# Two expert layers: unused single units load no weights, four leave the main run for a conditional block

## The chip, the core and the metric

The program runs on one core of one Trainium2 chip. The metric is device time in microseconds (us) of one execution. The core has five engines with queues of their own: TensorE (PE; its weight loads are listed as PEld), VectorE (DVE), ScalarE (ACT), GpSimd (POOL) and SyncE (SP). SP issues the plain transfers, POOL the indirect ones. An engine works through its queue in order and waits on semaphores.

## What is computed

Windowed attention, then two expert layers, on 7168 tokens of width 192. Layer one sends each token to two of eight experts, layer two to one.

```python
def reference(**kwargs):
    attn_out = _attn_ref(**attn_kwargs)             # seven last tokens, weights by softmax
    x = attn_out.reshape(B * S, D)
    x = _moe_ref(x=x, **moe_kwargs)                 # two experts a token, noisy gate
    return _moe2_ref(x=x, **moe2_kwargs)            # one expert a token, cosine router
...
            h = np.maximum(x[mask] @ w1[e], 0.0)    # 192 -> 1024
            out[mask] += top2_w[mask, k, None] * (h @ w2[e])   # 1024 -> 192
```

Which tokens an expert gets is known only on the chip. The reference's own routing of its inputs gives the experts of layer one 1867, 1722, 1777, 1820, 1775, 1810, 1732 and 1833 entries, those of layer two 1184, 1182, 2138, 279, 462, 463, 585 and 875.

## The kernel before

**Units.** A unit is 128 entries of one expert. Two units of one expert make a pair, and a tile of work is a pair or a single unit. The number of tiles is fixed when the program is built, with room for every routing: layer one has 56 pair slots and 8 single units, layer two 28 and 8. A single unit is for an expert with an odd number of units (or for a pair that found no slot). With the counts above the experts' units are 15, 14, 14, 15, 14, 15, 14, 15 and 10, 10, 17, 3, 4, 4, 5, 7. Each layer thus has four experts with an odd number and fills its pair slots (56 and 28) with the rest: units 0 to 3 of each layer hold entries, units 4 to 7 are computed on rows that are thrown away when they are written.

**A tile's steps.** `gather` (POOL, three tiles ahead) fetches the rows. `weights` (SP) fetches the expert's weights from DRAM (`WS`, names ws0 and ws1 for the two layers) in two parts: part 0, 4096 columns or 1024 KB, for the first product, and part 1, 3072 columns or 768 KB, for the second. `transp` turns the rows on PE. `first_product` (line L1028 in the profile, tile `ph`) is 40 matmuls, each of 256 columns in a pair and of 128 in a single unit. ACT and DVE make the hidden layer's two halves `hh` and `hl`. `second_product` (L1054, tile `py`) is 48 matmuls, or 24 in a single unit. ACT scales the result into `ys`, POOL scatters it. The first product of a tile is interleaved with the second of the tile before (`ORDER`).

**Weights and buffers.** Pairs use two buffers by turns, `wb[0]` and `wb[1]` (in the trace `wb`). All single units of both layers share a third that lies in the end of the input's tile (in the trace `xh`; its loads are the rows `xh<-ws`). Every load carries a condition, the integer `flag_i` of its slot:

```python
            e = SP.value_load(exec_i[l][0:1, c:c + 1], min_val=0, max_val=7)
            f = SP.value_load(flag_i[l][0:1, c:c + 1], min_val=0, max_val=1)
            loads.append(SP.dma_start(w[:, cols], WS[l][bass.ds(e * 128, 128), cols], cond=f))
```

For a pair the flag is one where its buffer passes to another expert. For all eight single units it is one (L688). `issue_after` keeps the loads in the order of the code, so a load that waits for its buffer holds up all later ones.

**Order.** `Layer` writes out the order of the tiles. Slots run in sections, as entries become known; the single units stand in the last section that still mixes all token groups, one behind each of its first eight pairs.

**Beside the tiles.** Routing, and the preparation of layer two's weights (L276 to L281 load `in_moe2_w1`, `in_moe2_w2` into a part of `xh`; L340 to L346 store them as ws1), are issued between the tiles by points in the program; their transfers share SP's queue with the loads. Tile i of the whole program is the i-th of layer one's 64 and layer two's 36.

Of the kernel before, what the change touches and what calls it, by code (L numbers as in the profile page):

```python
# [24 lines left out]
NS = 8  # L25
CB = 8
# [13 lines left out]
class Layer:  # L40
    """Static plan of one routed layer: k entries per token, column groups of tokens."""

    def __init__(self, k, groups, mixed):
        self.k, self.groups = k, groups
        self.np = N * k // 256
        self.cap = [b * 128 * k // 256 for _, b in groups]
        self.sec = [0] + [cdiv(b * 128 * k - E * 255, 256) for _, b in groups[:-1]]
        # mixed: the slot by which the entries of all groups but the last have been run
        self.done = [(groups[-2][1] * 128 * k + E * 255) // 256] if mixed else []
        # Each run of slots is taken from its start and from its middle by turns, one weight buffer for either,  # L50
        # so that a buffer is loaded anew only where its own half passes on to another expert.
        cuts = self.sec + self.done + [self.np]
        self.buf, self.fresh, order = {}, [], []
        for a, b in zip(cuts, cuts[1:]):
            m = a + cdiv(b - a, 2)
            self.fresh += [a, m]
            u = 0
            for j in range(b - a):
                s = (a, m)[j % 2] + j // 2
                self.buf[s] = len(self.buf) % 2  # L60
                order.append(("p", s))
                # the single units follow the first pairs that hold entries of every group
                left = NS - j
                if a == self.sec[-1] and 0 < left <= NS:
                    order.append(("s", u))
                    u += 1
        assert len(order) == self.np + NS
        self.order = order
        self.pos = {o: i for i, o in enumerate(order)}
        self.first = [self.pos[("p", s)] for s in self.sec]  # L70
        self.units = 2 * self.np + NS


@with_exitstack
def two_moe(ctx: ExitStack, tc: tile.TileContext, x, wgen, w_gate, w_noise, noise, w1a, w2a, emb, tau, w1b, w2b, out):
    nc = tc.nc
    L1 = Layer(2, G1, True)
    L2 = Layer(1, G2, False)
# [71 lines left out]
    # masks by partition: all, below 64, from 64 on  # L150
# [9 lines left out]
    # an entry's value: (1 + partition / 128) 2^(place - 56)  # L160
# [94 lines left out]
    @contextmanager  # L255
    def urgent(l):
        """work of a patient job that would wait for ever on an engine that is never idle."""
        low = tc.cur_priority
        if l:
            tc.cur_priority = state["here"]  # L260
        yield
        if l:
            state["here"] = tc.cur_priority
            tc.cur_priority = low
# [108 lines left out]
    def after_tile():  # L373
        """work beside a tile that stays behind the tile's own work that was issued before."""
        return tc.issue_after(state["pin"].ins) if "pin" in state else ExitStack()

    def after_product():
        """TensorE's work beside the tiles, which stays behind the products that were issued before."""
        return tc.issue_after(state["pe"].ins) if "pe" in state else ExitStack()
# [116 lines left out]
    def top1(v, m, dst, n):  # L496
        """dst: one-hot of the first largest of v; m: the largest."""
        t = rt.tile([128, E * GM], F32, name="rowt").rearrange("p (c e) -> p c e", e=E)[:, :n]
        mx = rt.tile([128, GM], F32, name="t1m")[:, :n]
        V.tensor_reduce(m, v, axis=AX.X, op=ALU.max)  # L500
        V.tensor_tensor(t, v, m[:, :, None].to_broadcast([128, n, E]), op=ALU.is_equal)
        yield 0.7
        V.tensor_mul(t, t, desc[:, None, :].to_broadcast([128, n, E]))
        V.tensor_reduce(mx, t, axis=AX.X, op=ALU.max)
        V.tensor_tensor(dst, t, mx[:, :, None].to_broadcast([128, n, E]), op=ALU.is_equal)
        yield 1.0
# [121 lines left out]
    def add_phase(l, lo, hi, at=None):  # L628
        """the pairs lo .. hi of every expert get the slots from `at` on, or those behind the phase before."""
        pn = plan[l]  # L630
        i = pn["rows"]
        w, inc = tn(f"w{l}{i}"), pn["end"][:, i]
        if lo is None:
            V.tensor_copy(w, hi)
        else:
            V.tensor_sub(w, hi, lo)
        prefix(inc, w)
        d = tn(f"d{l}{i}")
        V.tensor_sub(d, inc, w)
        base = float(at) if at is not None else pn["tail"]  # L640
        if base is not None:
            V.tensor_scalar(inc, inc, base, None, op0=ALU.add)
            V.tensor_scalar(d, d, base, None, op0=ALU.add)
        if lo is not None:
            V.tensor_sub(d, d, lo)
        V.tensor_scalar(d, d, 256.0, None, op0=ALU.mult)
        if lo is not None:
            df, cu = tn(f"df{l}{i}"), tn(f"cu{l}{i}")
            V.tensor_sub(df, d, tn(f"d{l}{pn['last']}"))
            V.tensor_scalar(cu, lo, 256.0, None, op0=ALU.mult)  # L650
        pn["last"], pn["tail"], pn["rows"] = i, inc[:, 7:8], i + 1
        return i

    def slot_experts(l, s0, s1):
        """the experts of pair slots s0..s1 (float)."""
        yield from threshold(l, iof[:, s0:s1], s1 - s0, exec_e[l][:, s0:s1])
# [20 lines left out]
    def exec_tables(l, a, b):  # L677
        """integer tables of the slots a..b: the expert, and whether the weights have to be loaded."""
        L = (L1, L2)[l]
        e, ei, fi = exec_e[l], exec_i[l], flag_i[l]  # L680
        V.tensor_copy(ei[:, a:b], e[:, a:b])
        c = min(b, L.np)
        V.tensor_tensor(fi[:, a + 1:c], e[:, a + 1:c], e[:, a:c - 1], op=ALU.not_equal)
        for s in L.fresh:
            if a <= s < c:
                V.memset(fi[:, s:s + 1], 1)
        if c < b:
            V.memset(fi[:, c:b], 1)  # L688
        yield 0.5
# [14 lines left out]
    def rows_of(dst, r, t, sh, phases, l, n):  # L704
        """rows of the ranks r of every expert, in the given phases."""
# [21 lines left out]
    def list_gen(l, L, g, row, n, nu, u0):  # L727
        """the entries of group g by row: onehots of a row's unit and place, multiplied."""
# [57 lines left out]
    def decode(l, v, n, us):  # L786
        """v: integers as floats, 128 (place + 71) + partition, or 0."""
# [20 lines left out]
    def left_over(l, L, g, lrow, fb, u0, nu):  # L808
        """adds the units that the section before g kept: full pairs in their place, and the rest, at the rows lrow."""
# [20 lines left out]
    def section_open(l, L, g, key):  # L830
        """full pairs of the tokens so far run; the rest of each expert is kept behind the last slot."""
# [48 lines left out]
    def left_ranks(l, g):  # L880
        """the ranks at which the two units begin that section g keeps of every expert."""
# [6 lines left out]
    def section_last(l, L, key):  # L888
# [11 lines left out]
        if L.done:  # L900
            # the pairs that end the entries of the groups before stand first
# [17 lines left out]
        def tables():  # L919
# [9 lines left out]
            yield 1.2  # L929
# [34 lines left out]
    live = {}  # L964

    def run_by(b):
        """the tile of layer one by which all entries of the tokens below column b have been run."""
# [15 lines left out]
    def slot(i):  # L983
        """a tile's place in the tables of its layer, and the weights it uses."""
# [3 lines left out]
    def weights(i, part):  # L988
        """part 0: the first product's weights, part 1: the second's."""
# [23 lines left out]
    def first_product(i, bg):  # L1013
        """in four parts, taken by turns with those of the second product of the tile before."""
# [137 lines left out]
    class Job:  # L1152
        """A generator of work with its key, the tile it may start after, and its place in the order of issue."""
# [15 lines left out]
    class Queue:  # L1169
        """Work beside the tiles: chains go one step a point, threads as far as their share of VectorE goes."""  # L1170
# [112 lines left out]
    for i in range(nt):  # L1283
        if i + LA < nt:
# [3 lines left out]
        one = first_product(i + 1, bgq.point) if i + 1 < nt else iter(())  # L1288
# [6 lines left out]
        if i + 3 < nt:  # L1295
            weights(i + 3, 0)
        bgq.at = i + 1
        if i + 2 < nt:
            weights(i + 2, 1)
        if i == C_AT:  # L1300
# [3 lines left out]
            state["last"] = True  # L1304

# [29 lines left out]
```

## Time and profile before

| | |
|---|---|
| time, median of 3 runs | 1094.52 us (1091.99 to 1097.86) |
| span of the profiled execution | 1096.0 us |
| PE busy | 946.8 us (86% of the span) |
| PEld busy | 853.9 us (78%) |
| DVE, ACT, POOL busy | 700.7, 605.3, 407.3 us |
| moved by DMA | 251.81 MB, mean 230 GB/s |
| mean granted clock of PE | 0.950 |

The table gives shares over the whole span. The program has stages with different limits (attention at the start, layer one, a passage in which layer one's results become layer two's inputs, layer two), so a share says little about one of them. The profiled execution has no time of its own on record beside its span; it lies 1.5 us above the median of the timed runs.

### The profile page before, as it was taken

Reading aid. Unit: us, or ns where it says so; the run is one execution under the profiler, and the core shown is the slowest. Engines: PE = TensorE matmul, PEld = TensorE weight load, DVE = VectorE, ACT = ScalarE, POOL = GpSimd, SP = SyncE. Lnnn points to the kernel's source line nnn. Section 1 sums busy time; section 2 is a strip of 40 time slices with the busy share of each in tenths; the row PEclk is TensorE's granted clock in tenths of the full one; section 3 lists DMA queues with packets and bytes.
Section 4 is the critical chain, followed back from the end, with each engine's and each line's share of the span. In section 5 each row is a group of like instructions: output and inputs, shape, how many; then the busy total and the mean of one; then the engine's idle time right before and its main releaser. Section 6 shows DMA issues by size and latency. Waiting matters only on the chain.

```text
span 1096.0 us, 27746 instructions
## 1 busy us (share of the span) xinstructions
PE 946.8 (86%) x10250; PEld 853.9 (78%) x10250; DVE 700.7 (64%) x1943; ACT 605.3 (55%) x1337; POOL 407.3 (37%) x384
## 2 busy tenths in 40 slices
PE   5891259899989999998989998988788999999996
PEld 2551248788878888998979897877678899999896
DVE  8996969889688979553434433988676733333331
ACT  2999336666465765555555543975265344444442
POOL 1000054443445454344334443333344444445422
PEclk9996569999999999999899999999899999999999
DMA  8789674556568564779798977866675736888751
GB/s 269 216 271 293 224 249 143 149 190 200 158 207 285 167 208 142 260 215 329 263 367 292 333 270 229 264 216 180 205 252 160 256 125 217 288 300 306 260 190 41
DMA packets 99464, 251.81 MB, mean 230 GB/s; under 512 B 14207, under 2 KB 65119, under 8 KB 89856
## 3 DMA queue, kind: packets, MB, share of 16 engines
q1 hardware_dynamic: 81664, 215.03, 57.9%
q0 software_dynamic: 17664, 35.01, 11.5%
q8 instruction: 80, 1.31, 0.5%
q14 instruction: 56, 0.46, 0.1%
HBM read 246.09 MB, written 58.69 MB: 278 GB/s over the span
## 4 chain that ended last, share of the span: by engine, by line
PE 32%; DMA 5%; issue 5%; DVE 3%; ACT 3%; POOL 3%; SPq 1%; another core or an unknown queue 1%; POOLq 0%; ACTq 0%
PE ph L1028 15%; PE py L1054 14%; DMA wb<-ws 3%; DMA xh<-ws 2%; PE pt L1006 1%; POOL xg L978 1%; PE bt L468 1%; POOL yb L1062 1%; ACT hh L1030 1%; POOL ss L536 1%; SPq L281 1%; ACT xt L473 1%; ACT xh L448 1%; PE bl L479 1%
## 5 line engine op out<-in xcount | busy, mean ns | idle before, releaser
L1028 PE MATMUL ph<-xt,wb 128*128 128x256 f16 x3360 | 422.6, 276 | 10.0 <-DVE hl L1031 4.1
L1054 PE MATMUL py<-wb,hh 128*128 128x192 f16 x2688 | 361.9, 248 | 17.9 <-ACT ys L1059 13.4
L1030 ACT ACTIVATE hh<-ph 128x512 f16<-128x512 f32 (+1 forms) x400 | 221.4, 560 | 269.7 <-PE ph L1028 209.7
L1028 PEld LDWEIGHTS <-wb 128*128 128x128 f16 x3360 | 327.3, 99 | 47.9 <-issue 9.7
L978 POOL DMA_INDIRECT xg<-t,gx x184 | 196.3, 1067 | 376.0 <-PE pt L1006 157.9
L1054 PEld LDWEIGHTS <-hh 128*128 128x128 f16 x2944 | 266.6, 99 | 28.0 <-issue 18.7
L1031 DVE SCALAR_TENSOR_TENSOR wt<-ph,hh 128x512 f16<-128x512 f32 x200 | 137.4, 689 | 116.6 <-ACT hh L1030 95.2
L1062 POOL DMA_INDIRECT yb<-ys,sx x120 | 131.5, 1096 | 198.0 <-ACT ys L1059 173.9
L1054 PE MATMUL py<-wb,wt 128*128 128x192 f16 x800 | 198.3, 248 | 0.2 <-issue 0.2
L1031 DVE SCALAR_TENSOR_TENSOR hl<-ph,hh 128x512 f16<-128x512 f32 (+1 forms) x200 | 118.9, 603 | 111.2 <-ACT hh L1030 87.6
L1054 PE MATMUL py<-wb,hl 128*128 128x192 f16 x544 | 134.9, 248 | 0.1
L1059 ACT ACTIVATE ys<-py,sc 128x192 f32<-128x192 f32 x184 | 68.0, 415 | 90.1 <-PE py L1054 74.3
L1062 POOL DMA_INDIRECT out_dram<-ys,sx x64 | 64.5, 1007 | 95.6 <-ACT ys L1059 83.5
L385 DVE TENSOR_TENSOR tmp<-xh,wt 128x768 f32<-128x768 f32 x90 | 84.9, 954 | 0.8 <-PE ph L412 0.7
L1054 PEld LDWEIGHTS <-wt 128*128 128x128 f16 x800 | 78.9, 99 | 0.8 <-issue 0.6
L1008 ACT ACTIVATE xt<-pt 128x768 f16<-128x768 f16 x84 | 67.7, 807 | 7.0 <-PE pt L1006 6.9
L1039 DVE TENSOR_SCALAR sc<-xg,csl 128x2 f32<-128x2 f32 (+1 forms) x100 | 23.0, 231 | 75.8 <-ACT ys L1059 60.2
L1054 PEld LDWEIGHTS <-hl 128*128 128x128 f16 x672 | 66.6, 99 | 0.2
L473 ACT ACTIVATE xt<-bt 128x768 f16<-128x768 f16 x56 | 45.2, 807 | 31.8 <-PE bt L468 21.9
L1006 PE MATMUL pt<-identh,xg 128*128 128x128 f16 x552 | 48.7, 222 | 11.6 <-DMA xg<-t,gx 11.4
L1028 PE MATMUL ph<-xt,xh 128*128 128x128 f16 x640 | 45.9, 223 | 7.4 <-DMA xh<-ws 4.7
L1006 PEld LDWEIGHTS <-xg 128*128 128x128 f16 x552 | 39.1, 99 | 14.4 <-DMA xg<-t,gx 11.9
(302 smaller groups left out, 1079.0 us busy)
## 6 DMA issues: line engine op xcount, KB each, us to landing
wb<-ws SPq DMA_DIRECT2D x84, 1024.0 KB
wb<-ws SPq DMA_DIRECT2D x84, 768.0 KB
xh<-ws SPq DMA_DIRECT2D x16, 1024.0 KB
ws<-wo SPq DMA_DIRECT2D x16, 768.0 KB
xh<-ws SPq DMA_DIRECT2D x16, 768.0 KB
tmp<-yb SPq DMA_DIRECT2D x28, 384.0 KB
ws<-wo SPq DMA_DIRECT2D x16, 512.0 KB
ws<-wo SPq DMA_DIRECT2D x32, 256.0 KB
```

The costliest lines, as they stand in the source:

```text
L385: V.tensor_mul(dst.rearrange("p t (h g) -> p (t h) g", g=G), xv, w)
L473: A.activation(xt.rearrange("p a n -> p (a n)"), pa[:, 0:768], AF.Copy)
L978: PL.indirect_dma_start(out=xg[:, h], out_offset=None, in_=T[l][0:rows_in], in_offset=bass.IndirectOffsetOnAxis(ap=gidx[l][:, u + h:u + h ...
L1006: PE.transpose(pt[:, j, h], xg[:, h, 128 * b:128 * b + 128], identh)
L1008: A.activation(xt.rearrange("p j h n -> p (j h n)"), pt.rearrange("p j h n -> p (j h n)"), AF.Copy)
L1028: state["pe"] = mark = PE.matmul(ph[:, q, :n], s, m, start=j == 0, stop=j == 4)
L1030: A.activation(hh[:, fs, :n], ph[:, :, :n], AF.Relu)
L1031: state["pin"] = V.scalar_tensor_tensor(hl[:, fs, :n], ph[:, :, :n], 0.0, hh[:, fs, :n], op0=ALU.max, op1=ALU.subtract)
L1039: V.tensor_scalar(sc[:, :nh], xg[:, :nh, 192:193].bitcast(F32).rearrange("p h o -> p (h o)"), csl[l][:, c:c + 1], None, op0=ALU.mult)
L1054: state["pe"] = PE.matmul(py[:, h], t[:, f, hs], w2[:, f, c], start=f == 0 and j == 0, stop=f == 7 and j == 2)
L1059: A.activation(ys[:, h], py[:, h], AF.Copy, scale=sc[:, h:h + 1])
L1062: d = PL.indirect_dma_start(out=dst, out_offset=bass.IndirectOffsetOnAxis(ap=sidx[l][:, u + h:u + h + 1], axis=0), in_=ys[:, h], in_offset ...
```

## The change

Four things change.

1. The flag of a single unit is computed on the chip: one if the unit holds entries, zero if not (`us`, two small DVE operations more in each layer, and a copy in place of a memset).
2. The single units stand spread over the section, not one behind each of its first pairs. Layer one keeps all eight in the main run, layer two the first four (`KEEP`).
3. Layer two's units 4 to 7 stand behind the main loop in a block that runs only if the flag of unit 4 is one. Inside, nothing is interleaved: gather, loads, transposes and products follow each other, tile by tile.
4. Every engine reads that flag into a register and branches on it. SP reads it earlier: its read stands ahead of part 0 of tile 73 (pair p7 of layer two), 23 tiles before the main run's end.

The order of the last mixed section, p for pairs and s for single units:

```
layer one, before: p33 s0 p40 s1 p34 s2 p41 s3 p35 s4 p42 s5 p36 s6 p43 s7 p37 p44 p38 p45 p39 p46
layer one, after:  p33 p40 s0 p34 p41 s1 p35 s2 p42 p36 s3 p43 s4 p37 p44 s5 p38 s6 p45 p39 s7 p46
layer two, before: p13 s0 p21 s1 p14 s2 p22 s3 p15 s4 p23 s5 p16 s6 p24 s7 p17 p25 p18 p26 p19 p27 p20
layer two, after:  p13 p21 p14 s0 p22 p15 p23 s1 p16 p24 p17 s2 p25 p18 p26 s3 p19 p27 p20 (block: s4 s5 s6 s7)
```

```diff
-                left = NS - j
-                if a == self.sec[-1] and 0 < left <= NS:
+                if a == self.sec[-1] and j + 1 >= cdiv((u + 1) * (b - a), spare + 1) and u < spare:
                     order.append(("s", u))
                     u += 1
+        self.main = len(order)
+        order += [("s", u) for u in range(spare, NS)]
...
-    L1 = Layer(2, G1, True)
-    L2 = Layer(1, G2, False)
+    L1 = Layer(2, G1, True, NS)
+    L2 = Layer(1, G2, False, KEEP)
...
         if c < b:
-            V.memset(fi[:, c:b], 1)
+            V.tensor_copy(fi[:, c:b], tn("us"))
...
+            us = tn("us")
+            V.scalar_tensor_tensor(us, sp, pn["tail"], m8, op0=ALU.is_ge, op1=ALU.mult)
+            V.tensor_scalar(us, us, -1.0, 1.0, op0=ALU.mult, op1=ALU.add)
+            yield 1.6
...
+    nm = base2 + L2.main
...
-    for i in range(nt):
-        if i + LA < nt:
+    for i in range(nm):
+        if i + LA < nm:
...
+    with tc.If(nc.values_load(flag_i[1][0:1, L2.np + KEEP:L2.np + KEEP + 1], min_val=0, max_val=1) > 0):
+        loads.clear()
+        for i in range(nm, nt):
+            gather(i)
+            for part in range(2):
+                weights(i, part)
+            transp(i)
+            for step in (first_product, second_product):
+                for _ in step(i, lambda share: None):
+                    pass
```

**SP in layer one, first place.** Behind the preparation's stores and loads for layer two (ws1, in_moe2_w1) stood, before, part 0 of p34 (wb1), part 1 of s1 (xh), part 0 of s2 (xh), part 1 of p34 (wb1) and part 0 of p41 (wb0). Rows that read registers are left out.

```order
L346 DMA ws1<-wo_8294 64x2048 x3
L276 DMA xh_73<-in_moe2_w1_dram 128x1024 x2
L278 DMA xh_73<-in_moe2_w1_dram 64x1024 x2
...
L996 DMA wb1_131<-ws0 128x4096
...
L996 DMA xh_73<-ws0 128x3072
...
L996 DMA xh_73<-ws0 128x4096
...
L996 DMA wb1_131<-ws0 128x3072
...
L996 DMA wb0_130<-ws0 128x4096
```

Now part 0 of p41 (wb0) stands right behind the same transfers, then part 1 of p34 (wb1), part 0 of s1 (xh), part 1 of p41 (wb0) and part 0 of p35 (wb1).

```order
L349 DMA ws1<-wo_8298 64x2048 x4
L279 DMA xh_73<-in_moe2_w1_dram 128x1024 x2
L281 DMA xh_73<-in_moe2_w1_dram 64x1024 x2
...
L1004 DMA wb0_130<-ws0 128x4096
...
L1004 DMA wb1_131<-ws0 128x3072
...
L1004 DMA xh_73<-ws0 128x4096
...
L1004 DMA wb0_130<-ws0 128x3072
...
L1004 DMA wb1_131<-ws0 128x4096
```

The eight transfers of the preparation stay where they were; a load of p41 has come to stand next behind them, and the loads of s1 and s2 have moved back.

**SP in layer one, second place.** Behind two transfers that fetch in_moe2_w2 stood part 0 of s5 (xh) and part 1 of p42 (wb0); ahead of them part 0 of p42 (wb0) and part 1 of s4 (xh).

```order
L996 DMA wb0_130<-ws0 128x4096
...
L996 DMA xh_73<-ws0 128x3072
L340 DMA ws1<-wo_9213 128x3072
L281 DMA xh_73<-in_moe2_w2_dram 128x8x192 x2
...
L996 DMA xh_73<-ws0 128x4096
...
L996 DMA wb0_130<-ws0 128x3072
```

Now part 0 of p43 (wb0) and part 1 of s3 (xh) stand there, and ahead of them part 0 of s3 (xh) and part 1 of p36 (wb1).

```order
L1004 DMA xh_73<-ws0 128x4096
...
L1004 DMA wb1_131<-ws0 128x3072
L343 DMA ws1<-wo_9215 128x3072
L284 DMA xh_73<-in_moe2_w2_dram 128x8x192 x2
...
L1004 DMA wb0_130<-ws0 128x4096
...
L1004 DMA xh_73<-ws0 128x3072
```

A unit without entries (s5) stood behind the two transfers, a pair stands there now.

**POOL at the end of the program.** Before, the last scatters (out_0) were followed by the end of the program.

```order
L1062 DMA out_0_dram<-ys_19620,sx1_171 7168x192 x2
L1062 DMA out_0_dram<-ys_19779,sx1_171 7168x192 x2
L1062 DMA out_0_dram<-ys_19919,sx1_171 7168x192 x2
L1062 DMA out_0_dram<-ys_20005,sx1_171 7168x192 x2
L1330 UNCONDITIONAL_BRANCH
L1330 ISA
```

Now the flag is read behind the last scatter of the main run, and the branch skips the block's four gathers (xg) and four scatters.

```order
L1070 DMA out_0_dram<-ys_19490,sx1_171 7168x192 x2
L1314 TENSOR_LOAD fi1_165
L1314 COMPARE_AND_BRANCH
L986 DMA xg_19562<-t1,gx1_169 128x196
...
L1070 DMA out_0_dram<-ys_20053,sx1_171 7168x192
L1314 UNCONDITIONAL_BRANCH
L1314 ISA
L1314 UNCONDITIONAL_BRANCH
L1349 ISA
```

A register read, a branch and a wait on POOL's own transfers have come between the last scatter and the end.

## Rows read from the trace of the kernel before

**Rows 1.** Span, granted clock (die median left out), and the page's busy shares.

```profile
core 0: 1096.0 us, clock 0.950
...
PE 946.8 (86%) x10250; PEld 853.9 (78%) x10250; DVE 700.7 (64%) x1943; ACT 605.3 (55%) x1337; POOL 407.3 (37%) x384
```

**Rows 2.** Windows of layer two: four pairs; then four pairs and four singles.

```profile
core 0: us, PE busy (x) PEld busy (x) DVE busy (x) ACT busy (x) POOL busy (x), PEclk, DMA share, GB/s
879.93:914.57 34.64, 34.64 (x378) 32.83 (x377) 11.98 (x20) 15.28 (x28) 13.91 (x15) 1.00 0.50 156
944.62:996.79 52.17, 52.17 (x646) 50.36 (x645) 19.17 (x40) 24.29 (x52) 23.78 (x24) 1.00 0.87 290
```

**Rows 3.** Windows, same columns: layer one's singles, its two waits, layer two's last singles.

```profile
501.20:616.90 115.70, 104.75 (x1202) 98.49 (x1199) 45.49 (x101) 59.66 (x126) 47.53 (x48) 0.94 0.91 325
515.00:527.00 12.00, 8.63 (x61) 7.35 (x60) 2.53 (x5) 6.08 (x13) 3.00 (x3) 0.72 0.75 270
567.50:588.00 20.50, 15.77 (x170) 14.88 (x168) 8.50 (x22) 12.77 (x27) 6.00 (x7) 0.83 0.84 304
996.79:1040.06 43.27, 41.94 (x488) 39.58 (x487) 15.45 (x30) 19.32 (x39) 20.70 (x21) 1.00 0.78 273
```

**Rows 4.** PE's waits from 501.2 to 616.9: us in total, times, longest.

```profile
PE ph L1028 <- DMA xh<-ws: 4.7, 1, 4.7
PE py L1054 <- DMA xh<-ws: 3.4, 1, 3.4
```

**Rows 5.** PE's timeline at the two waits: start, us, instructions, idle before.

```profile
520.42 0.50 PE L1054 MATMUL py<-xh,hh 128*128 128x192 f16 x2 [3.37 <-DMA xh<-ws]
...
573.11 1.14 PE L1028 MATMUL ph<-xt,xh 128*128 128x128 f16 x9 [4.73 <-DMA xh<-ws]
```

**Rows 6.** SP's timeline ahead of the two waits: start, us to the group's end.

```profile
501.64 2.00 SPq L346 DMA_DIRECT2D ws<-wo  x3
503.68 1.36 SPq L276 DMA_DIRECT2D xh<-in_moe_w_dram  x2
505.08 3.69 SPq L278 DMA_DIRECT2D xh<-in_moe_w_dram  x2
510.28 0.10 SPq L996 DMA_DIRECT2D wb<-ws  x1
...
554.70 7.06 SPq L281 DMA_DIRECT2D xh<-in_moe_w_dram  x2
563.34 2.02 SPq L996 DMA_DIRECT2D xh<-ws  x1
```

**Rows 7.** The chain that ended last, from 490 to 640: start, us, what.

```profile
511.95 8.42 DMA xh<-ws
...
563.34 9.73 DMA xh<-ws
```

**Rows 8.** The page's transfers that single units issue, over the whole span.

```profile
xh<-ws SPq DMA_DIRECT2D x16, 1024.0 KB
...
xh<-ws SPq DMA_DIRECT2D x16, 768.0 KB
```

**Rows 9.** SP's register reads of a flag (ns min/median/max), and the instruction queue.

```profile
L995 SPq TENSOR_LOAD <-fi x200: 3/268/1560, 137.9 to 1067.0; - x100
...
q8 instruction: 80, 1.31, 0.5%
```

**Rows 10.** DVE writes layer two's last flags; SP's first load behind the new read's place.

```profile
857.60 0.17 DVE L683 TENSOR_TENSOR fi<-xe 128x14 int32<-128x14 f32 x1
...
858.07 0.06 DVE L686 MEMSET fi<- 128x1 int32 x1
...
871.78 0.08 SPq L996 DMA_DIRECT2D wb<-ws  x1
```

**Rows 11.** The end of the span: timeline of POOL, with ACT's last result.

```profile
1088.11 0.73 ACT L1059 ACTIVATE ys<-py,sc 128x192 f32<-128x192 f32 x2 [4.26 <-issue]
...
1090.09 0.98 POOL L1062 DMA_INDIRECT out_dram<-ys,sx  x1 [0.30 <-issue]
```

More of the change, by code (lines that the diff above doesn't have):

```diff
@@ L25 @@
 NS = 8
+KEEP = 4
 CB = 8
@@ L40, with __init__ @@
 class Layer:
-    def __init__(self, k, groups, mixed):
+    def __init__(self, k, groups, mixed, spare):
         self.k, self.groups = k, groups
@@ L928, in tables @@
             V.tensor_scalar(m8, iof[:, 0:8], so[:, 7:8], None, op0=ALU.is_ge)
-            yield 1.2
+            us = tn("us")
+            V.scalar_tensor_tensor(us, sp, pn["tail"], m8, op0=ALU.is_ge, op1=ALU.mult)
+            V.tensor_scalar(us, us, -1.0, 1.0, op0=ALU.mult, op1=ALU.add)
+            yield 1.6
             yield from threshold(l, sp, 8, q2)
@@ L1287, in two_moe @@
             gather(i + LA)
-        one = first_product(i + 1, bgq.point) if i + 1 < nt else iter(())
+        one = first_product(i + 1, bgq.point) if i + 1 < nm else iter(())
         two = second_product(i, bgq.point)
@@ L1294, in two_moe @@
                 pass
-        if i + 3 < nt:
+        if i + 3 < nm:
             weights(i + 3, 0)
         bgq.at = i + 1
-        if i + 2 < nt:
+        if i + 2 < nm:
             weights(i + 2, 1)
```

## The prediction

> **What bounds the kernel now.** I read the page's shares and the granted clock first [rows 1]: PE is busy for 86% of the span at a mean clock of 0.95, so it is the engine to follow, stage by stage. Windows come next. In layer two there is a stretch of four pairs, and one of four pairs with four single units, in which PE's busy time is the whole window at clock 1.00 [rows 2]. Nothing waits there; time is matmuls. A pair takes 34.64 / 4 = 8.66 us, and a single unit (52.17 - 34.64) / 4 = 4.38 us.
>
> Layer one's stretch of single units is another matter [rows 3]: 115.70 us, of which PE is busy for 104.75 at a clock of 0.94. So 10.95 us are idle, and (1 - 0.94) x 115.70 = 6.9 us go to the lower clock, 17.9 us in all above the work itself. The waits of PE say where [rows 4]: two waits for weights of single units make 8.1 of the 10.95. The timeline puts them at 517.05 to 520.42 and 568.38 to 573.11 [rows 5]. The reader is to see in rows 3 that the clock is 0.72 and 0.83 in the windows around just these two. With the clock the first costs 3.37 + 0.28 x 12.0 = 6.7 us and the second 4.73 + 0.17 x 20.5 = 8.2 us, together 14.9; the other 3.0 us are crumbs.
>
> Why those loads came late is read on SP [rows 6, 7]. The first one left at 511.95, behind seven transfers that prepare layer two's weights (an eighth, a store, left before the piece shown), and landed 8.42 us later. The second left at 563.34, after two such transfers had held SP for 7.06 us, and landed 9.73 us later.
>
> **The change, part by part.**
>
> *Layer two loses four units.* With the counts in the document exactly units 0 to 3 hold entries, so unit 4's flag is zero and the block is skipped. Four times 4.38 us of PE's work go, in a stretch where PE's busy time is the window: 17.5 us. No wait can swallow it there unless a new one arises. The loads get rarer (eight units' loads in one stretch before, four over a longer one now), at a DMA share that was already 0.87 without a wait.
>
> *Layer two's last waits.* From 996.79 to 1040.06 PE idles 43.27 - 41.94 = 1.33 us [rows 3]. Spread units leave more room between loads; between 0 and 1.3 us, and I take 1.3.
>
> *Layer one loads less.* All eight units are still computed, so PE's work stays. Of the 16 loads of either size that units make [rows 8], layer one's units 4 to 7 drop four of each; a load of both parts is 1.75 MB, so some 7.3 MB of 0.325 x 115.70 = 37.6 MB in the stretch [rows 3]. What this is worth is the 14.9 us of the two waits, and each has to be followed into the new order.
>
> First wait. The preparation's eight transfers stay, and right behind them comes part 0 of p41, a real load (p41 is the first slot of another expert), where before stood one of p34 that its flag skips. If it leaves at 510.28, where that one left, and takes 8.42 us, it is there at 518.7. Ahead of p41's first product now stand three first products (p40, s0, p34), as many as stood ahead of s1's second product (s0, p40, s1) with a part of p34's interleaved; so it is wanted at about 517. A wait of 1.7 us is left, half of 3.37. I let half of its cost stay, 3.4 us. What is late is then a pair, no longer a single unit.
>
> Second wait. The load that was late belongs to s5, and s5 is not in use: it is gone. Behind the two transfers now stands part 0 of p43. Ahead of p43 there is one pair more and one single unit fewer than ahead of s5, so it is wanted 8.66 - 4.38 = 4.3 us later, less the 3.3 us won before: at about 569.4. The two transfers are held by p36's part 1, ahead of which there is one pair more and two single units fewer than ahead of s4's: no difference (8.66 - 8.76), so they leave 3.3 us earlier and the load lands at 573.1 - 3.3 = 569.8. A wait of 0.4 us. I let 1.0 us stay.
>
> So layer one gives 14.9 - 3.4 - 1.0 = 10.5 us. The ends: nothing, if pairs wait as units did; 17.9, if every wait and all of the lower clock go. The passage to layer two keeps its order apart from one preparation store that moved behind p47's load, and comes earlier as a whole.
>
> *The end.* POOL reads the flag behind its last scatter, branches and waits for its own transfers before the end. The last scatter's issue ends at 1090.09 + 0.98 = 1091.07, 4.9 us before the span does [rows 11]. A flag read takes 0.27 us in the median, 1.56 at most [rows 9]. From below: 0.3 us, if the rest lies beside the 4.9 us that pass anyway; from above 5 us, if these start anew. I take 1.5, nearer to the read's row. The other engines are done earlier: ACT's last result ends at 1088.84. If POOL did not end last, their reads would be what counts.
>
> No row shows a taken branch. The instruction queue's row has 80 packets in 0.5% of 16 engines' span [rows 9], so 0.005 x 16 x 1096.0 / 80 = 1.1 us a packet. The Trainium skill ("Runtime: NRT & Kernel Launch", section "Instruction fetch mechanics") speaks against a branch: a taken one whose target lies outside the pages on hand has to fetch its page first. By the rule the end costs a packet more, 1.5 + 1.1 = 2.6 us, and the sum would be 1067.8; by the rows alone it is as below. No run so far shows which.
>
> *At nothing.* DVE's two added operations are of the size of the flag's own (0.17 us) [rows 10], on an engine that is busy for 64% [rows 1]; without cover they cost 0.7 us in all. SP's early read of the flag stands ahead of a load that leaves at 871.78, since its buffer is busy until then; the flags are written behind 858.07 [rows 10]. It costs nothing as long as these 13.7 us last; a later flag would hold up the loads of p7 and all pairs behind it.
>
> *The sum*, against the profiled span: 1096.0 - 17.5 - 1.3 - 10.5 + 1.5 = 1068.2 us. The median of the timed runs lies 1.5 us below the span, so 1066.7.
>
> **The rivals.**
>
> *The waits only move.* p41 and p43 are loads of 1.75 MB that stand behind the same transfers as s1 and s5 did, and pairs can't do without theirs. For it speaks that the DMA share is 0.91 over the stretch [rows 3]; against it, that it was 0.75 in the window of the first wait, so bandwidth was not what lacked, and that the second load is not needed any more. Layer one then gives nothing: 1068.2 + 10.5 - 1.5 = 1077.2 us.
>
> *All waits go.* With 7.3 MB less the whole 17.9 us go and the end costs 0.3: 1096.0 - 17.5 - 1.3 - 17.9 + 0.3 - 1.5 = 1058.1 us. Against it: the preparation's transfers stay where they are, and some crumbs are not loads.
>
> *The block runs* (the other side). If unit 4's flag is one, because a fifth unit holds entries or because the flag comes out wrong, the change does not do what it says: four units run one after the other behind the main run, each with the landing of its part 0 (8.42 us [rows 7]) and its products, uncovered, at no less than twice 4.38 us, since neither half hides the other's hand-over: 17.2 us a unit, 68.7 in all, so 1066.7 + 68.7 = 1135.4 us. It decides from the fifth unit in use on. Against it stand the counts: four odd numbers of units, 28 pairs for 28 slots.
>
> **How the numbers follow.** The forecast has 0.60, the moved waits 0.20, the full gain 0.15, the block 0.03; 0.02 is left for a mishap that eats the gain. 1067 us is the likeliest case. From 1057 to 1079 the range holds the forecast and, with a margin of 1 to 2 us, the two cases beside it; the block is left out. About 0.5% (5.5 us) is what a measurement of this kernel can tell from no change. All cases but the last two are faster by far more: faster 0.95, within 0.5% 0.02, slower 0.03.
>
> **What would show it.** Right: `xh<-ws` issues in the executed main run fall from 16 to 12 of either size, single-unit first-product matmuls from 640 to 480, PE's busy time by about 17 us or more. Layer two's stretch from p13 on is four times 4.38 us shorter, without a wait. In layer one no wait for `xh` weights of more than 1 us is left, and the clock is 1.00 in most of the stretch; a wait for `wb` weights of some 2 us stands at p41. The stretch from the first behind p33 to p37 is shorter by about 10 us. From the last scatter to the end pass about 6 us. Wrong: matmuls of the block behind the last pair; waits of 3 us and more for `wb` in layer one; SP standing at the early flag read; or a tail of 10 us behind the last scatter.

## The result and the profile after

| | before | after |
|---|---|---|
| time, median (4 runs each, taken together) | 1095.15 us (1091.99 to 1097.86) | 1067.32 us (1067.20 to 1071.42) |
| after / before, 95% interval | | 0.9755 (0.9735 to 0.9774) |
| span of the profiled execution | 1096.0 us | 1065.6 us |

The change made the kernel faster by 27.8 us; 1067 us, with a range of 1057 to 1079, was forecast. Timed again later beside another set of runs of the kernel before, it stood at 0.9745 (0.9718 to 0.9771).

These rows of the page after answer to [rows 1, 8]:

```profile
PE 925.9 (87%) x9982; PEld 834.4 (78%) x9982; DVE 694.5 (65%) x1927; ACT 594.8 (56%) x1313; POOL 394.7 (37%) x376
...
xh<-ws SPq DMA_DIRECT2D x12, 1024.0 KB
xh<-ws SPq DMA_DIRECT2D x12, 768.0 KB
```

Both counts came as forecast: 16 to 12 loads of either size, and TensorE's busy time 20.9 us lower.

Where the time came from is read from four windows of either execution, cut at the ends of the second products of p32 and p47 of layer one and p12 and p20 of layer two, so that the same work stands in each apart from what was dropped. Columns as in [rows 2]: the stretch, its us, busy us of the engines, granted clock, DMA share, GB/s. Before:

```profile
494.70:678.10 183.40, 172.09 (x1957) 162.63 (x1955) 72.68 (x154) 92.71 (x189) 78.87 (x79) 0.96 0.87 300
678.10:925.00 246.90, 216.23 (x2485) 196.30 (x2483) 171.21 (x677) 137.28 (x346) 95.27 (x84) 0.96 0.66 211
925.00:1088.00 163.00, 160.80 (x1898) 153.55 (x1895) 56.12 (x109) 71.54 (x147) 66.23 (x67) 1.00 0.69 237
1088.00:1096.00 8.00, 0.02 (x1) 0.00 (x0) 0.00 (x0) 0.73 (x2) 1.96 (x2) 0.81 0.05 15
```

After:

```profile
494.40:666.20 171.80, 166.66 (x1953) 158.45 (x1952) 73.61 (x155) 90.89 (x190) 77.87 (x78) 1.00 0.80 278
666.20:911.10 244.90, 216.40 (x2486) 196.55 (x2484) 171.39 (x679) 138.16 (x346) 95.23 (x86) 0.97 0.64 208
911.10:1054.50 143.40, 142.58 (x1627) 135.89 (x1624) 49.10 (x89) 61.46 (x123) 56.46 (x57) 1.00 0.63 223
1054.50:1065.60 11.10, 0.00 (x1) 0.00 (x0) 0.00 (x0) 0.73 (x2) 1.96 (x2) 0.74 0.05 14
```

Layer one's stretch of single units gave 11.6 us (10.5 forecast), layer two 19.6 (18.8 forecast), the passage between them 2.0 (nothing forecast), the part ahead of the first window 0.3, and the end cost 3.1 (1.5 forecast): 30.4 us between the spans.

For layer one, these windows of after answer to [rows 3]:

```profile
501.20:616.90 115.70, 111.32 (x1336) 105.99 (x1334) 49.71 (x111) 62.89 (x133) 50.81 (x52) 1.00 0.87 305
515.00:527.00 12.00, 10.32 (x115) 9.49 (x113) 5.21 (x14) 7.53 (x15) 4.38 (x5) 1.00 0.92 368
567.50:588.00 20.50, 19.13 (x223) 17.81 (x222) 11.60 (x27) 14.37 (x32) 8.15 (x8) 1.00 0.90 289
```

In the same 115.70 us TensorE is busy for 6.6 us more, and the clock, which was 0.72 and 0.83 around the two waits, is 1.00 in all three windows. DMA moves 305 GB/s, where it moved 325 before. The waits of TensorE from 494 to 667 us answer to [rows 4]:

```profile
PE ph L1036 <- issue: 1.9, 2, 1.7
...
PE ph L1036 <- DMA wb<-ws: 0.3, 1, 0.3
```

No wait for unit weights (`xh`) is in this list any more. The 1.7 us are p41's; SyncE's timeline, the chain of work and TensorE's timeline show them; they answer to [rows 5 to 7]:

```profile
498.55 3.80 SPq L349 DMA_DIRECT2D ws<-wo  x4
502.40 2.41 SPq L279 DMA_DIRECT2D xh<-in_moe_w_dram  x2
504.85 1.27 SPq L281 DMA_DIRECT2D xh<-in_moe_w_dram  x2
507.87 2.00 SPq L1004 DMA_DIRECT2D wb<-ws  x2
```

```profile
507.87 8.88 DMA wb<-ws
516.75 1.20 issue
517.95 2.36 PE ph L1036 x20
```

```profile
517.95 2.36 PE L1036 MATMUL ph<-xt,wb 128*128 128x256 f16 x20 [1.68 <-issue]
```

Behind the preparation's eight transfers p41's part 0 leaves at 507.87, and the last record of its landing is 8.88 us later, at 516.75. TensorE had stopped at 516.27 (517.95 - 1.68), so 0.48 us of the wait lie ahead of that record and 1.20 us behind it; the latter are why the wait is put down to "issue". Before, the two late products started 0.05 us and less behind their loads' landings [rows 5, 7]. So whether the 1.20 us are the load's as well stays open.

The end is read from the branch's line on the sequencers (PEldq is TensorE's; ns min/median/max, first and last start) and from the line that ends the program:

```profile
L1314 PEldq COMPARE_BRANCH  x1: 3770/3770/3770, 1053.6 to 1053.6; - x1
...
L1314 POOLq TENSOR_LOAD <-fi x1: 507/507/507, 1055.7 to 1055.7; - x1
L1314 POOLq COMPARE_BRANCH  x1: 45/45/45, 1056.2 to 1056.2; - x1
...
L1314 POOLq INC_SWDGE_SEM  x1: 1019/1019/1019, 1060.2 to 1060.2; - x1
...
L1349 POOLq DRAIN  x3: 45/107/3495, 1061.3 to 1065.3; - x3
```

The same last line of the kernel before:

```profile
L1330 POOLq DRAIN  x3: 45/107/6057, 1089.2 to 1095.8; - x3
```

Before, GpSimd's drain of 6.06 us began at 1089.2, 0.9 us ahead of the last scatter's issue at 1090.09 [rows 11], and ran beside it. After, GpSimd issues its last scatter at 1056.57, waits at the end of the skipped block until 1060.2, and only then, from 1061.3, drains for 3.50 us.

### The profile page after: what moved, and what is told of

It reads as the page before. It is cut to its first block, busy times and chain, and to the rows that moved or that the text cites. A ratio compares the mean times of both kernels' runs of the same rounds, so it can differ in the third digit from the quotient of the medians.

```text
span 1065.6 us, 27079 instructions
## 1 busy us (share of the span) xinstructions
PE 925.9 (87%) x9982; PEld 834.4 (78%) x9982; DVE 694.5 (65%) x1927; ACT 594.8 (56%) x1313; POOL 394.7 (37%) x376
## 4 chain that ended last, share of the span: by engine, by line
PE 52%; DVE 24%; ACT 8%; issue 7%; DMA 5%; POOL 2%; SPq 1%; another core or an unknown queue 1%; ACTq 0%; POOLq 0%; DVEq 0%
PE ph L1036 23%; PE py L1062 21%; DVE tmp L388 3%; DVE hl L1039 3%; DVE wo L339 2%; DVE wt L1039 2%; DVE acc L403 2%; PE pt L1014 2%; PE bt L471 2%; ACT wo L337 1%; PE bl L482 1%; DMA wb<-in_moe_w_dram 1%; ACT hh L1038 1%; DMA xg<-t,gx 1%; PE bl L763 1%
## 5 line engine op out<-in xcount | busy, mean ns | idle before, releaser
L1038 ACT ACTIVATE hh<-ph 128x512 f16<-128x512 f32 (+1 forms) x384 | 216.4, 568 | 261.0 <-PE ph L1036 191.3
L986 POOL DMA_INDIRECT xg<-t,gx x180 | 188.3, 1046 | 342.9 <-PE pt L1014 135.5
L1062 PEld LDWEIGHTS <-hh 128*128 128x128 f16 x2880 | 260.4, 99 | 17.5 <-issue 13.8
L1039 DVE SCALAR_TENSOR_TENSOR wt<-ph,hh 128x512 f16<-128x512 f32 (+1 forms) x192 | 127.1, 665 | 115.7 <-ACT hh L1038 88.5
L1039 DVE SCALAR_TENSOR_TENSOR hl<-ph,hh 128x512 f16<-128x512 f32 (+1 forms) x192 | 122.5, 643 | 102.6 <-ACT hh L1038 77.0
L1062 PE MATMUL py<-wb,wt 128*128 128x192 f16 x704 | 173.3, 246 | 0.9 <-issue 0.9
L1062 PE MATMUL py<-wb,hl 128*128 128x192 f16 x640 | 160.0, 250 | 1.0 <-issue 1.0
L1070 POOL DMA_INDIRECT out_dram<-ys,sx x60 | 61.0, 1016 | 103.0 <-ACT ys L1067 93.5
L1062 PEld LDWEIGHTS <-wt 128*128 128x128 f16 x736 | 72.0, 98 | 0.0
L1014 PE MATMUL pt<-identh,xg 128*128 128x128 f16 x540 | 46.6, 220 | 10.6 <-DMA xg<-t,gx 10.4
L1014 PEld LDWEIGHTS <-xg 128*128 128x128 f16 x540 | 37.7, 98 | 13.1 <-DMA xg<-t,gx 10.9
L337 ACT ACTIVATE wo<-xh,wsc 128x384 f16<-128x384 f32 (+1 forms) x70 | 41.9, 654 | 10.4 <-DVE wsc L242 9.8
```

Source lines behind the costliest of these rows:

```text
L337: A.activation(h, v, AF.Copy, scale=sc[:, c:c + 1])
L986: PL.indirect_dma_start(out=xg[:, h], out_offset=None, in_=T[l][0:rows_in], in_offset=bass.IndirectOffsetOnAxis(ap=gidx[l][:, u + h:u + h ...
L1014: PE.transpose(pt[:, j, h], xg[:, h, 128 * b:128 * b + 128], identh)
L1038: A.activation(hh[:, fs, :n], ph[:, :, :n], AF.Relu)
L1039: state["pin"] = V.scalar_tensor_tensor(hl[:, fs, :n], ph[:, :, :n], 0.0, hh[:, fs, :n], op0=ALU.max, op1=ALU.subtract)
L1062: state["pe"] = PE.matmul(py[:, h], t[:, f, hs], w2[:, f, c], start=f == 0 and j == 0, stop=f == 7 and j == 2)
```

## The experiments

The runs were made in three sets on different chips, each beside runs of the kernel before: its median was 1095.29 and 1095.54 us in the first and third set and 1071.36 us in the second. So ratios are compared across sets, and times only within one. The change's own runs, made ahead of these sets, stood beside a median of 1095.15 us, so its 1067.3 us can be set beside the times of the first set. Waits and stretches are those of one execution of each kernel.

**Order and loads of layer one apart (three kernels, first set).** In the first, layer one has its old order, with the missing loads kept:

```diff
-if a == self.sec[-1] and j + 1 >= cdiv((u + 1) * (b - a), spare + 1) and u < spare:
+if a == self.sec[-1] and u < spare and (j + 1 >= cdiv((u + 1) * (b - a), spare + 1) or k == 2):
```

> The changed kernel, with layer one's eight units back in the old dense order (one behind each pair from p33 on); units not in use still load nothing. Theory (two waits, each behind preparation transfers; the spread order shortens the first, the missing load removes the second): the first wait is back at s1, 3.4 us with a clock near 0.72 around it, in place of 1.7 us at clock 1.00, and the second stays away, so 1067.3 + 6.7 - 1.7 = 1072.3 us. Rival A (the order does it all: a unit behind every pair leaves no time for the next load, used or not): both waits return, 1067.3 + 11.6 = 1078.9 us. Rival B (the missing loads do it all): 1067.3 us, no wait over 2 us.

In the second, the order is spread and all eight units load:

```diff
-            V.tensor_copy(fi[:, c:b], tn("us"))
+            if l == 0:
+                V.memset(fi[:, c:b], 1)
+            else:
+                V.tensor_copy(fi[:, c:b], tn("us"))
```

> The changed kernel with layer one's eight units spread as in it, but all eight load their weights. Theory (the missing load removes the second wait): the second wait comes back with s4's or s5's load, some 8.2 - 1.0 us with its clock: 1067.3 + 7.2 = 1074.5 us. Rival A (the room that the spread order leaves does it all): within 2 us of the changed kernel, at most 1069.3 us, no wait for unit weights over 1 us. Rival B (the 7.3 MB more hold everything up): over 1078.9 us, as much as the whole gain of the stretch, 11.6 us.

The third has both edits.

> The changed kernel with both parts of layer one undone: dense order, all eight units load; layer two and the conditional block as in the change. Theory: both waits are back and the layer is as before, 1067.3 + 11.6 = 1078.9 us, and 1080.9 if the 2.0 us that the passage to layer two gained hang on layer one's order. With the two kernels above it tells whether order and loads add up (5.0 + 7.2 = 12.2 us for the theory) or either alone would have done (rivals A and B: one of them is worth 11.6 and the other nothing).

| layer one | ratio to before (95%) | median, us | stretch p32 to p47, us |
|---|---|---|---|
| spread, unused units don't load (the change) | 0.9755 (0.9735 to 0.9774) | 1067.3 | 171.8 |
| spread, all load | 0.9753 (0.9727 to 0.978) | 1066.6 | 171.7 |
| dense, unused units don't load | 0.9791 (0.977 to 0.9812) | 1072.7 | 177.3 |
| dense, all load | 0.9852 (0.9826 to 0.9878) | 1077.9 | 181.1 |

With all loads, dense, TensorE's timeline has both waits:

```profile
519.56 0.34 PE L1065 MATMUL py<-xh,hh 128*128 128x192 f16 x2 [4.69 <-DMA xh<-ws]
...
570.08 2.25 PE L1039 MATMUL ph<-xt,xh 128*128 128x128 f16 x29 [3.59 <-DMA xh<-ws]
```

Dense without the unused loads, only the first is left:

```profile
520.24 0.50 PE L1062 MATMUL py<-xh,hh 128*128 128x192 f16 x2 [4.45 <-DMA xh<-ws]
```

Spread with all loads, neither; the longest wait is p41's, again put down to issue. Behind the two transfers of the second place the load of p43 stands next there too, and its product waits for 0.80 us:

```profile
515.11 2.36 PE L1039 MATMUL ph<-xt,wb 128*128 128x256 f16 x20 [1.43 <-issue]
...
566.96 2.36 PE L1039 MATMUL ph<-xt,wb 128*128 128x256 f16 x20 [0.80 <-DMA wb<-ws]
```

In the dense order the missing loads are worth 5.2 us and take the second wait away, as the theory had it (1072.3 expected, 1072.7 measured). But in the spread order they are worth nothing: rival A of the second kernel, against the theory's 1074.5. The order alone takes both waits away and is worth 11.3 us. The two parts don't add up, since either is enough for the second wait.

**The preparation's transfers moved (third set).** Dense order and all loads, and the job that prepares layer two's weights pauses for two tiles more, so that its group of seven transfers stands ahead of s3's load on SyncE's queue.

```diff
-                if self.threads[2]:
+                if self.threads[2] and not 33 <= self.at <= 35:
```

> The kernel with layer one's dense order and all eight loads, in which the group of seven transfers that prepare layer two's weights waits for two tiles more: on SyncE's queue it stands ahead of part 0 of s3's load, no longer ahead of p34's and s1's. Theory (the first wait is the group's, which holds the queue in front of a unit's load): the wait of 4.7 us at s1's second product goes, and one of 2 to 5 us stands at s3 or the pair behind it (p41). Rival (the wait is the dense order's: a unit's buffer comes free too late for the next unit's load, whatever else is on the queue): 3 us and more still at s1. The place of the wait decides, the time should stay within 4 us of the kernel without the shift.

TensorE's timeline now has its two waits for unit weights here:

```profile
537.17 3.27 PE L1039 MATMUL ph<-xt,xh 128*128 128x128 f16 x29 [5.41 <-DMA xh<-ws]
...
597.02 3.15 PE L1039 MATMUL ph<-xt,xh 128*128 128x128 f16 x29 [2.67 <-DMA xh<-ws]
```

They are s3's and s7's; s1 and s5, which waited before, don't. SyncE's timeline has the group just ahead of the first load, and the two transfers of in_moe2_w2, which the pause moved too, just ahead of the second:

```profile
518.04 3.05 SPq L349 DMA_DIRECT2D ws<-wo  x3
521.13 1.07 SPq L279 DMA_DIRECT2D xh<-in_moe_w_dram  x2
522.24 1.50 SPq L281 DMA_DIRECT2D xh<-in_moe_w_dram  x2
525.29 0.35 SPq L1007 DMA_DIRECT2D xh<-ws  x1
...
580.21 4.76 SPq L284 DMA_DIRECT2D xh<-in_moe_w_dram  x2
587.11 1.65 SPq L1007 DMA_DIRECT2D xh<-ws  x1
```

So in the dense order the waits go where the transfers go: they are the transfers', and the theory holds (the spread order was not tried with the group moved). The time does not: 0.9938 (0.9918 to 0.9958), some 9 us over the kernel without the shift (0.9852), where at most 4 were expected. The stretch is only 1.1 us longer (182.2 against 181.1); the passage behind it is 14:

```profile
674.80:932.20 257.40, 219.10 (x2486) 198.79 (x2485) 171.89 (x679) 138.51 (x346) 94.40 (x86) 0.92 0.61 199
```

Without the shift it took 243.30 us at a clock of 0.97. That the preparation then ends too late for layer two is likely, but was not shown.

**The old orders with the flags alone (second set).** The kernel before, in which units not in use load nothing; no block, eight units in layer two.

```diff
-            V.memset(fi[:, c:b], 1)
+            V.tensor_copy(fi[:, c:b], tn("us"))
```

> The kernel before with one part of the change alone: units not in use load nothing; both old orders, no block, all eight units of layer two computed. Theory (from the runs so far: missing loads are worth 5.2 us in layer one's dense order, and at most 1.3 in layer two): 1095.3 - 5.2 - 1.3 = 1088.8 us; in layer one the first wait (3.4 to 4.7 us) stands, the second is gone. Rival A (the loads were the trouble throughout): 1095.3 - 11.6 - 1.3 = 1082.4 us. Rival B (nothing without the new order): 1095 us.

The ratio is 0.9948 (0.993 to 0.9966), on 1095.3 us 1089.6, next to the theory's 1088.8 and away from both rivals. In its trace a wait of 2.4 us stands at s1's second product and, just ahead, one of 2.0 us for a pair's weights; the second wait is gone.

This run also says what took layer two's last wait away. Before, from 925 to 1090 us, TensorE waited once for weights there, and they were a pair's:

```profile
PE py L1054 <- DMA wb<-ws: 1.1, 1, 1.1
```

With the flags alone no wait for weights is left in that stretch, though all eight units stand there in the old order, and the stretch from p12 to p20 takes 161.70 us where it took 163.00:

```profile
894.40:1056.10 161.70, 160.41 (x1897) 153.53 (x1894) 55.69 (x109) 73.01 (x147) 66.22 (x67) 1.00 0.59 194
```

That is 1.3 us for the loads that are not made.

**Layer two's kept units dense (second set).**

```diff
-if a == self.sec[-1] and j + 1 >= cdiv((u + 1) * (b - a), spare + 1) and u < spare:
+if a == self.sec[-1] and u < spare and (j + 1 >= cdiv((u + 1) * (b - a), spare + 1) or k == 1):
```

> The changed kernel with layer two's four kept units in the old dense order (one behind each of p13, p21, p14, p22); everything else as in the change. Theory (spreading them took away layer two's last waits): 1.3 us come back, 1068.6 us, and the stretch from p12's last product to p20's takes 144.7 us in place of 143.4. Rival (those waits hung on the units that are not in use, whose loads are gone): 1067.3 us, 143.4 us in the stretch. The stretch decides, the time of a run varies by more than this.

```profile
889.80:1033.40 143.60, 142.73 (x1630) 136.04 (x1626) 48.81 (x89) 63.43 (x123) 58.35 (x59) 1.00 0.63 215
```

The stretch takes 143.60 us in the old order; in the new one it takes 143.40, in the change and in the kernel of the same set whose block runs: the rival. In layer two the order is worth nothing; the last wait there went with the loads of the four units, as the run with the flags alone shows. The ratio, 0.9768 (0.9745 to 0.9792), is too wide to tell.

**No block (first set).** The `tc.If` and what stands in it are left out.

> The changed kernel without its conditional block: layer two's units 4 to 7 are left out of the program (with these inputs they hold nothing). Theory (the end is longer because the wait for the last scatter and the drain stand one behind the other after the branch, where they overlapped before): the 3.1 us of the end come back, 1067.3 - 3.1 = 1064.2 us, with 8.0 us from the last pair's products to the end. Rival (the longer end comes from the last scatter itself, which lands 1.5 us later): no more than 1 us comes back, 1066.3 to 1067.3 us, and the end keeps 10 to 11 us. Second rival (TensorE's slow branch of 3.8 us holds the end): the same 3.1 us come back, but then the last engine to finish in the changed kernel would be TensorE, which was done 8 us before the end.

```profile
1055.50:1062.80 7.30, 0.00 (x0) 0.00 (x0) 0.00 (x0) 0.73 (x2) 1.96 (x2) 0.68 0.05 17
```

```profile
L1338 POOLq DRAIN  x3: 45/107/5402, 1056.6 to 1062.6; - x3
```

The end takes 7.30 us (11.10 and 11.40 in two executions of the changed kernel), and the drain starts beside the last scatter again. The time fell by 2.1 us, to 1065.2 (0.9732, 0.9708 to 0.9756); the intervals overlap, so the window decides: 3.8 us, the theory's mechanism at a little more than its price.

**The block runs (second set).**

```diff
+            if l == 1:
+                V.memset(fi[:, c + KEEP:c + KEEP + 1], 1)
```

> The changed kernel with unit 4's flag of layer two set to one, so that the conditional block runs (its four units hold nothing; unit 4 loads weights, the others don't). The price of a fifth unit in use. Theory: four units one after the other, twice 4.38 us each for products that hide nothing, and one load of 8.4 us and more ahead of the first: 4 x 8.76 + 8.4 = 43.4 us, less the 3.1 us at most that the end restarts anyway: 1067.3 + 40 to 43 = 1107 to 1111 us. Rival A, the upper bound of the forecast (a landing's time for every unit, loaded or not): 1067.3 + 68.7 = 1136.0 us. Rival B (the four units pipeline as in the main run): 1067.3 + 17.5 + 8.4 = 1093.2 us.

```profile
1036.30:1072.30 36.00, 19.61 (x268) 18.86 (x268) 7.64 (x20) 10.29 (x26) 9.78 (x10) 0.83 0.12 16
```

```profile
PE pt L1016 <- DMA xg<-t,gx: 9.6, 3, 7.0
```

The ratio is 1.0008 (0.999 to 1.0026), on 1095.3 us 1096.2: rival B's 1093.2 is nearest, theory and upper bound fall. The end took 36.0 us, 25 more than skipped (10.9 in the run with layer two's units dense, of the same set). Of these TensorE waited 9.6 us for gathered rows and was busy for 19.6 with four units' products, one close behind the other; 6.8 us passed behind the last product. Unit 4's weights were not waited for: SyncE, which reads the flag early, entered the block at 1023.2, 13 us ahead of this window. A fifth unit in use thus costs about all that the change brings.

**A block in layer one too (second and third set).** Units 4 to 7 of layer one in a block of their own, ahead of p46's second product and p47's first; in the second version units 0 to 3 stand at the places that they have in the change.

```diff
-    L1 = Layer(2, G1, True, NS)
+    L1 = Layer(2, G1, True, KEEP)
...
+    for n, i in enumerate(seq):
+        after = dict(enumerate(seq[n:]))
+        if 1 in after and after[1] == rest[0][-1] + 1:
+            block(0)
```

> The changed kernel, with layer one's units 4 to 7 in a conditional block of their own too, ahead of p46's second product and p47's first; units 0 to 3 spread over the stretch. Theory (TensorE pays the flag's load and a taken branch, 0.59 + 3.77 us as at the end of the changed kernel, and about 1 us of hand-over, all else goes on in time): 1067.3 - 17.5 + 5.4 = 1055.2 us. Rival A (SyncE waits at the block for all its transfers to land, so the next pairs' weights are late): 3 to 9 us more, 1058 to 1064 us, with waits for wb weights at p47 or p52. Rival B (the branch costs nothing in mid-program): 1050 to 1051 us.

> Both blocks, with layer one's units 0 to 3 at the places they have in the changed kernel (spread as if eight were kept), since in the first version with both blocks a wait of 3.55 us for unit weights had come back at s2. Theory (that wait, with a clock of 0.96 over 40 us around it, goes; the branch's 5.3 us and the products that nothing hides at the block stay): 4 to 5 us below the first version, which stood at 0.9758 of the kernel before: 0.971 to 0.972, 4 us below the changed kernel. Rival (the passage to layer two swallows what the stretch ahead of it gains, as it swallowed 3 of 5 us in the first version): 0.975, no gain on the changed kernel.

> The changed kernel once more, unaltered, as the measure for the two kernels timed beside it (the kernel before took 1095.3 us in one set of runs and 1071.4 in another, so times of different sets can't be set against each other). Expected: 0.9755 of the kernel before, as at first, within 0.002.

The first version came to 0.9758 (0.973 to 0.9787), so its theory and both rivals, 1050 to 1064 us or 0.959 to 0.971, fall. The second came to 0.9727 (0.9704 to 0.9751) beside the change's 0.9745 (0.9718 to 0.9771): no gain that can be told. Its theory (0.971 to 0.972, 4 us below the change) and its rival (0.975, none) both stay possible: the ratio lies nearer to the theory, the 1.1 us between the medians of the two kernels nearer to the rival. The wait for unit weights at s2 did go, but waits of 4.1 us for pairs' weights came. TensorE's waits and the windows of the second version say where four units' 17.5 us stay:

```profile
PE ph L1052 <- PEq L1310: 5.6, 1, 5.6
PE ph L1052 <- DMA wb<-ws: 4.1, 2, 2.9
PE ph L1052 <- issue: 3.5, 5, 1.1
```

```profile
493.20:661.00 167.80, 154.08 (x1686) 143.03 (x1684) 66.52 (x135) 83.27 (x165) 69.22 (x70) 0.96 0.80 286
661.00:906.00 245.00, 214.25 (x2487) 196.22 (x2485) 171.82 (x679) 138.94 (x346) 94.99 (x86) 0.96 0.64 207
```

The stretch is only 2.6 us shorter than the change's beside it (170.4): 5.6 go to the branch (L1310), other waits and a lower clock take most of the rest. The passage, 241.7 us in the change's execution beside it, took 245.0. Whether it would have been longer anyway is open: with nothing in it changed, it took between 241.7 and 247.5 us in the executions of the changed kernel and of the one without its block.

## Why the prediction was right, step by step

*The sum was right partly by luck.* It gave a span of 1068.2 us and a median 1.5 below. The span came out at 1065.6, and the median 1.7 above it: the changed kernel's profiled execution has a time of its own, 1067.37 for the span of 1065.6, so 1.8 us lie around a span. The profiled execution of before therefore stood at about 1097.8, the top of its runs' range. Two errors of about 3 us cancelled.

*Layer two, 17.5 and 1.3.* Measured 19.6: TensorE's busy time in the stretch fell by 18.2 (160.80 to 142.58) and its idle time by 1.4. The units' price was about right, and so was the size of the second term. But the 1.3 us were put down to the room between loads, and that step failed: the dense order gives 143.6 us as well, and with the flags alone the missing loads bring the 1.3 us in the old order.

*Layer one, 10.5 of 14.9.* Measured 11.6 in the window, and 10.6 in time between the two kernels that differ in layer one alone (1077.9 and 1067.3). First wait: p41 waited 1.68 us where 1.7 was worked out, which is partly luck. The load was to leave at 510.28, to land at 518.7 and to be wanted at about 517; it left at 507.87, the last record of its landing is at 516.75, and it was wanted at 516.27. By these records it was 0.48 us late, and the other 1.20 us stay open. That the wait of before was the group's is shown by the moved group. Oversized was the price of what stays: half of the cost with its clock (3.4), while the clock stayed at 1.00 and the wait cost itself. In a second execution of the changed kernel no wait over 0.6 us stood there. Second wait: it went, and of the 0.4 us worked out for p43 0.34 were measured. But "the load is not needed" is only one of two sufficient reasons: the order alone removes the wait, with s5's load made.

*The end, 1.5 between 0.3 and 5.* Measured 3.1 in the change, 3.8 against the kernel without the block. The upper bound's mechanism ("if these start anew") is the true one, and the value was taken from the wrong end: not the flag's read but GpSimd's wait for its own scatters and the drain behind it are the price. About 6 us from the last scatter to the end were forecast, 8.0 were measured (1057.55 to 1065.6).

*The taken branch.* On TensorE it took 3.77 us (the first 0.9 of them beside its last products), on the other engines 0.05 to 0.07. Where the block ran, the same branch and the one behind it took TensorE 0.09 and 0.18 us:

```profile
L1316 PEldq COMPARE_BRANCH  x2: 87/134/180, 1035.4 to 1064.5; - x2
```

So leaving out the block is what costs, and on the engine that has by far the most instructions in it (268 matmuls against 10 to 26 instructions of the others in the window above). The DMA queues of the changed kernel show a transfer of instructions while TensorE stands at its branch, from 1053.6 to 1057.4 (packets, MB, share):

```profile
q8 instruction: 1, 0.02, 2.1%
```

This packet lasts from 1054.66 to 1055.91, and the branch ends 1.4 us behind it. Each of the eleven taken branches of TensorE in the traces has one such packet, which ends 1.4 to 1.5 us ahead of the branch's end, whether the branch takes 3.33 us or 6.30; at the branches not taken there is none. This agrees with the rule of the Trainium skill ("Runtime: NRT & Kernel Launch", section "Instruction fetch mechanics") that a taken branch out of the pages on hand must fetch its target first.

The 1.1 us that the forecast worked out for a packet are near the 1.25 measured, but the branch takes three times as long. At the end of the program its 3.77 us cost nothing, since TensorE was through at 1057.4 and GpSimd at 1064.8; the forecast's 2.6 us for the end with a packet came nearer to 3.1 for another reason. In mid-program the branch took 6.0 and 6.3 us, and TensorE stood idle for 5.3 and 5.6 of them. The packet started 3.6 and 3.9 us behind the branch there, against 1.0 to 1.6 at the end of the program; that is where the longer time lies.

*The passage, nothing.* It gave 2.0 us, which is less than two executions of one order differ by there (241.7 and 244.9). It can't be put down to the change.

*The rivals.* Moved waits would have given 1077.2, and 1077.9 is what layer one's old order with all loads takes. That all waits go, 1058.1, did not come true: 5.1 us of layer one's stretch (171.80 less 166.66 busy) are still idle. The block that runs was priced at 68.7 us; it costs 25 over the skipped one. The 17.2 us a unit had counted a landing and doubled products for each, while no landing of weights was waited for and the four units' products took TensorE 19.6 us together.

## What to carry to other kernels

In this kernel a wait behind a fixed group of transfers shrank or went when the first consumer behind the group stood further off; to learn whether a wait is a group's, move the group and see whether the wait follows. Two edits that each remove the same wait must be tried apart and together, since their gains don't add. Price a skipped block by what stands behind its join (an engine's wait for its own transfers, a drain that starts anew) and by the branch on the engine with the most instructions in the block, with a look at the instruction queue while it lasts. In mid-program the branch and the waits that came with it ate nearly all of the work that the block saved.

## What was not expected of the hardware

TensorE's taken branch took 3.77 us at the end of the program and 6.0 to 6.3 us in the middle, against 0.09 not taken, and each time a transfer of instructions ended 1.4 to 1.5 us ahead of its end. And the same kernel before took 1095.3 us on one chip and 1071.4 on another, 2.2% apart, more than most of the edits here are worth.
